# Attention and a gated feed-forward layer in one kernel: first weights cast in row halves on three engines, two gates before two values in tile 0, and a last store of 128 columns

## The chip, the cores and the metric

The kernel runs on one core of a Trainium2 chip. A time is the device time in microseconds (us) of one execution. The kernel before took 367.27 us, the median of 3 runs (366.66 to 367.38). Each timing batch runs the kernel before and the others on the same chip in turn. Each trace is of one execution.

## The reference

Blockwise causal attention (8 batches, 8 heads, 576 positions of 64 elements) is followed by a gated feed-forward layer. Cut to what matters:

```python
scores = (q @ k.T) / 8            # masked: 64-row block i sees blocks j <= i
x = softmax(scores) @ v           # regrouped to 4608 tokens x 512
gate = maximum(x @ w_gate, 0)     # 512 x 1536
val  = x @ w_val                  # 512 x 1536
out  = (gate * val) @ w_out       # 1536 x 512, float32
```

## The kernel before

All inputs are float32 in memory, and the products run in bfloat16. The 4608 tokens form nine tiles of 512. Tiles 0 to 7 are the first 512 positions of a batch; tile 8 gathers the last 64 positions of all batches. TensorE (PE) runs a hand-made order in which attention of later batches is woven between products of the current tile. What bears on the change is the start, where PE must wait for inputs and weights, and the end.

The casts of the weights: a *half* holds 256 of the 1536 columns, for gate and value. One tile is 128 partitions x 4 row chunks x 256 columns, 512 KB as float32. GpSimd (POOL) casts each whole.

```python
def load_w_half(i, g):
    ...                                    # cut: one DMA each for wg and wv, 512 KB
    sts.append((dst[i][:, :, 256 * g : 256 * g + 256], st))
    return sts

def cast_w(sts, eng):
    for dst, st in sts:
        eng(dst, st)
```

The products of a tile come from a generator; each `next` emits one matmul, 512 columns wide. Tiles 0 and 1 start with f = 0 and 1 together, so that chunk c, which comes from head pair c, is wanted late. The rest of the tile takes one f at a time, four gate products and then four value products. PSUM, where products accumulate, has three buffers in `psum_ffn`, one in `psum_one` and two in `psum_sc`.

```python
for f in range(first, 12):
    gate = psum_ffn.tile([128, 512], FP, name="ffnp")
    val = psum_ffn.tile([128, 512], FP, name="ffnp")
    steps = [(t, c) for t in range(2) for c in range(4)]
    if (j, f) == (0, 8):
        steps.sort(key=lambda e: e[1] // 2)
    for t, c in steps:
        product((gate, val)[t], t, c, f)
        if (t, c) == (0, 3):
            gate_sb = relu(gate)           # ScalarE (ACT), 0.60 us
        if (t, c) == (1, 3):
            hidden(gate_sb, val)           # VectorE (DVE), writes hT
        yield
```

The start of the program. The head pairs are counted from 0. `both_av(3)` is the product with v of the fourth pair (pair 3), `to_xT_pe(3, ..)` transposes its result, and the c = 3 products need that.

```python
cast_w(w_0[0][:1], pool)
corners(3, zero_pool)
cast_w(w_0[0][1:], pool)
ffn(4)
to_xT_pe(2, act)
both_av(3)
ffn(5)
to_xT_pe(3, dve)
cast_w(w_0[1], pool)
...
ffn(23)
```

The end. The last output group of tile 8 is cut in two column halves. Each evacuation (`ob`) is followed by two stores of 64 rows, one issued by ACT and one by SyncE (SP).

```python
def outs(j):
    full = [(s, 0, 512) for s in range(4)]
    return full if j < B else full[:3] + [(3, 0, 256), (3, 256, 512)]
```

The softmax here doesn't subtract the row's maximum and nothing guards it: scores larger than these inputs give would overflow.

## Time and profile before

| reading | view | value |
|---|---|---|
| span of the profiled run | page | 364.3 us |
| PE busy, PE's share of the chain | page | 97%, 88% |
| four 512-column matmuls, start to start | timeline of PE | 0.864 us |
| first product of the feed-forward layer | timeline of PE | 16.72 us |
| product f = 10 of tile 0 | timeline of PE | 35.79 us |
| third output group of tile 0 | timeline of PE | 48.37 us |
| evacuation of the last output columns starts | timeline of DVE | 360.47 us |

These are lines of the page of the kernel before: busy time of engines with their share of the span, the clock granted to TensorE in 40 slices (tenths of full speed), shares of the chain that ended last, and the group of the gate products.

```profile
PE 354.9 (97%) x2963; PEld 175.8 (48%) x2963; DVE 168.7 (46%) x393; ACT 168.4 (46%) x278; POOL 113.7 (31%) x147
...
PEclk9999999999999999999999999999999999999999
...
PE 88%; DMA 6%; ACT 2%; DVE 2%; issue 0%; POOL 0%; ACTq 0%
...
L585 PE MATMUL ffnp<-xT,wg 128*128 128x512 bf16 x384 | 103.6, 380 | 0.4 <-POOL wg L340 0.3
```

PE is busy nearly all the time, and PE work makes up nearly all of the chain. The group's idle time before it is only 0.4 us in all, for 384 recorded matmuls. So there is little to gain, and it lies in single gaps. The next lines are from the timeline of PE of the kernel before. Columns: start (us), duration of the row (us), engine, source line, operation, output and inputs, shapes, count. A bracket at the end gives the idle time before the row and what ended it.

```profile
15.97 0.47 PE L508 MATMUL ffnp<-v_bf,attnT 128*128 128x65 bf16 x10
16.72 1.04 PE L585 MATMUL ffnp<-xT,wg 128*128 128x512 bf16 x4 [0.29 <-POOL wg L340]
...
20.58 0.59 PE L585 MATMUL ffnp<-xT,wg 128*128 128x512 bf16 x2
...
21.22 0.38 PE L585 MATMUL sc<-xT,wv 128*128 128x512 bf16 x1
21.64 1.02 PE L585 MATMUL ffnp<-xT,wg 128*128 128x512 bf16 x4
22.58 1.04 PE L585 MATMUL ffnp<-xT,wv 128*128 128x512 bf16 x4
...
32.95 0.59 PE L585 MATMUL ffnp<-xT,wg 128*128 128x512 bf16 x2
33.62 0.60 PE L585 MATMUL ffnp<-xT,wv 128*128 128x512 bf16 x2
...
35.79 0.38 PE L585 MATMUL ffnp<-xT,wg 128*128 128x512 bf16 x1
...
48.37 0.59 PE L646 MATMUL ffnp<-wo,hT 128*128 128x512 bf16 x2 [0.17 <-DVE ob L656]
```

Four gaps can be read. (1) The first product, at 16.72, waits for POOL's cast of wg. (2) The third gate starts at 21.64, where the single product before it (21.22, at 0.216 a product) ended its turn at 21.44. (3) The values that follow start at 22.58, and the four gates before them need only 0.864 from 21.64, so to 22.50. (4) The row at 33.62 comes 0.67 after the row at 32.95, which has two products and needs 0.43. Later, at 48.37, the third output group waits 0.17 for DVE.

The end, from the timeline of DVE of the kernel before, shows the last three evacuations:

```profile
357.85 0.69 DVE L656 COPY ob<-ffnp 128x512 f32<-128x512 f32 x1 [1.90 <-PE ffnp L646]
359.16 0.42 DVE L656 COPY ob<-ffnp 128x256 f32<-128x256 f32 x1 [0.62 <-PE ffnp L646]
360.47 0.42 DVE L656 COPY ob<-ffnp 128x256 f32<-128x256 f32 x1 [0.89 <-PE ffnp L646]
```

### The profile page before, as it was taken

How to read it: one execution, taken by the hardware profiler on the slowest of the kernel's cores; microseconds unless marked ns; L12 is line 12 of the kernel's file. 1: busy time of each engine (PE TensorE's matmuls, PEld its weight loads, DVE VectorE, ACT ScalarE, POOL GpSimd, SP SyncE). 2: the span in 40 equal slices, each digit the busy share in tenths (PEclk: the TensorE clock that was granted, in tenths of full speed). 3: DMA queues.
4: the chain of work that ended last, by engine and by line, in shares of the span. 5: the costliest groups of instructions: out<-in, count | busy, mean ns of one | idle time of the engine just before them, and what ended most of it. 6: DMA issues, size and time to landing. Idle time of an engine off the chain costs nothing.

```text
span 364.3 us, 7455 instructions
## 1 busy us (share of the span) xinstructions
PE 354.9 (97%) x2963; PEld 175.8 (48%) x2963; DVE 168.7 (46%) x393; ACT 168.4 (46%) x278; POOL 113.7 (31%) x147
## 2 busy tenths in 40 slices
PE   6899999999999999999999999999999999999995
PEld 2544455544545445444544454445544454444443
DVE  4744455475534553454454434543455434333332
ACT  4833564677146634664256624564355333302310
POOL 6756656489129100850058003900000000000000
PEclk9999999999999999999999999999999999999999
DMA  7999999999999962999379963999100320020013
GB/s 253 287 356 375 315 248 298 251 94 139 154 183 142 144 144 81 81 134 175 113 50 141 142 146 53 137 127 167 64 17 14 74 81 0 0 88 29 0 45 102
DMA packets 150340, 49.58 MB, mean 136 GB/s; under 512 B 132769, under 2 KB 143265, under 8 KB 150305
## 3 DMA queue, kind: packets, MB, share of 16 engines
q0 software_dynamic: 70320, 8.85, 52.1%
q1 hardware_dynamic: 74704, 31.08, 41.3%
q10 hardware_dynamic: 5280, 9.18, 7.8%
q8 instruction: 23, 0.38, 0.4%
q14 instruction: 13, 0.10, 0.1%
HBM read 37.75 MB, written 9.44 MB: 130 GB/s over the span
## 4 chain that ended last, share of the span: by engine, by line
PE 88%; DMA 6%; ACT 2%; DVE 2%; issue 0%; POOL 0%; ACTq 0%
PE ffnp L585 47%; PE ffnp L646 26%; PE ffnp L508 5%; PE sc L395 3%; PE ffnp L488 3%; DMA stage<-in_moe_w_gate_dram 3%; DMA stage<-in_moe_w_val_dram 3%; PE one L395 2%; ACT attnT L368 1%; PE sc L429 1%; DMA stage<-in_q_dram 1%; DVE qTm L248 1%; PE ffnp L239 0%; PE one L429 0%; ACT kTm L248 0%
## 5 line engine op out<-in xcount | busy, mean ns | idle before, releaser
L601 DVE TENSOR_TENSOR hT<-gate_sb,ffnp 128x512 bf16<-128x512 bf16 x106 | 72.7, 686 | 95.7 <-PE ffnp L585 76.8
L595 ACT ACTIVATE gate_sb<-ffnp 128x512 bf16<-128x512 f32 x108 | 64.8, 602 | 100.0 <-PE ffnp L585 99.9
L585 PE MATMUL ffnp<-xT,wg 128*128 128x512 bf16 x384 | 103.6, 380 | 0.4 <-POOL wg L340 0.3
L646 PE MATMUL ffnp<-wo,hT 128*128 128x512 bf16 (+1 forms) x444 | 101.4, 374 | 0.2 <-DVE ob L656 0.2
L585 PE MATMUL ffnp<-xT,wv 128*128 128x512 bf16 x376 | 101.0, 380 | 0.1
L585 PEld LDWEIGHTS <-wg 128*128 128x128 bf16 x432 | 40.1, 98 | 46.6 <-issue 3.7
L585 PEld LDWEIGHTS <-wv 128*128 128x128 bf16 x432 | 39.7, 98 | 46.0 <-issue 2.3
L646 PEld LDWEIGHTS <-hT 128*128 128x128 bf16 x444 | 40.8, 98 | 42.0 <-issue 1.1
L404 ACT ACTIVATE attnT<-sc 128x1024 bf16<-128x1024 f32 x56 | 57.0, 1042 | 0.0
L282 POOL DMA_DIRECT2D q_bf<-in_q_dram x20 | 18.2, 930 | 94.2 <-DVE hT L601 80.2
L656 DVE COPY ob<-ffnp 128x512 f32<-128x512 f32 (+1 forms) x37 | 25.0, 677 | 41.4 <-PE ffnp L646 41.3
L508 PEld LDWEIGHTS <-attnT 128*128 128x128 bf16 x640 | 26.0, 98 | 14.4 <-DVE xnat L474 3.8
L473 DVE RECIPROCAL recip<-ffnp 128x4 f32<-128x4 f32 (+1 forms) x73 | 13.1, 179 | 35.1 <-PE ffnp L508 23.4
L508 PE MATMUL ffnp<-v_bf,attnT 128*128 128x65 bf16 x570 | 26.4, 194 | 0.0
L410 ACT ACTIVATE attnT<-one 128x256 bf16<-128x256 f32 x28 | 10.7, 384 | 32.6 <-PE ffnp L395 30.1
L474 DVE TENSOR_TENSOR xnat<-ffnp,recip 128x256 bf16<-128x256 f32 x57 | 24.2, 424 | 2.0
L282 POOL DMA_DIRECT2D v_bf<-in_v_dram x25 | 21.4, 944 | 0.0
L450 ACT ACTIVATE attnTt<-one 64x256 bf16<-64x256 f32 x8 | 3.0, 377 | 36.0 <-PE ffnp L429 36.0
L282 POOL DMA_DIRECT2D k_bf<-in_k_dram x20 | 17.8, 942 | 0.0
L395 PE MATMUL sc<-qTm,kTm 64*128 64x512 bf16 (+1 forms) x168 | 17.2, 305 | 0.4 <-ACT kTm L248 0.4
L395 PEld LDWEIGHTS <-kTm 64*128 64x128 bf16 x224 | 9.2, 94 | 16.2 <-issue 11.7
L441 ACT ACTIVATE attnTt<-sc 128x1024 bf16<-128x1024 f32 x16 | 15.7, 1016 | 0.0
(89 smaller groups left out, 241.3 us busy)
## 6 DMA issues: line engine op xcount, KB each, us to landing
out_dram<-ob ACTq DMA_DIRECT2D x32, 256.0 KB, 2.5
stage<-in_moe_w_gate_dram SPq DMA_DIRECT2D x6, 512.0 KB, 9.0
stage<-in_moe_w_val_dram SPq DMA_DIRECT2D x6, 512.0 KB, 9.1
stage<-in_moe_w_out_dram SPq DMA_DIRECT2D x6, 512.0 KB, 10.5
q_bf<-in_q_dram POOLq DMA_DIRECT2D x20, 128.0 KB, 4.6
k_bf<-in_k_dram POOLq DMA_DIRECT2D x20, 128.0 KB, 5.7
v_bf<-in_v_dram POOLq DMA_DIRECT2D x20, 128.0 KB, 5.9
stage<-in_v_dram SPq DMA_DIRECT2D x19, 128.0 KB, 4.4
```

What stands on the lines that cost most here:

```text
L282: ins = nc.gpsimd.dma_start(dst, src[b, :, 128 * c : 128 * c + n, :].rearrange("h p d -> p h d"),)
L395: nc.tensor.matmul(where[c].rearrange("p (c n) -> p c n", n=128), kTm[b % 2][head_of(hh), c, hp, :], qTm[b % 2][head_of(hh), c:4, hp, :], ...
L404: return lambda: nc.scalar.activation(at[:, :, lo : lo + 512], sc, AF.Exp, scale=scale)
L441: return lambda: nc.scalar.activation(at[:, :, 2 * i : 2 * i + 2, 0:256], main[i].rearrange("p g (h n) -> p g h n", h=2), AF.Exp, scale=scale,
L473: nc.vector.reciprocal(recip, av[:, :, 64])
L474: nc.vector.tensor_tensor(out=out, in0=av[:, :, 0:64], in1=recip.to_broadcast([rows, n, 64]), op=AX.mult,)
L508: nc.tensor.matmul(av[:, p, :], at[:, col : col + 128], v_bf[b % 2][:, c, h, :], start=(p == 0), stop=(c == p), skip_group_check=True,)
L585: nc.tensor.matmul(to, (wg, wv)[t][f // 4][:, c, 128 * (f % 4) : 128 * (f % 4) + 128], x[:, c], start=(c == 0), stop=(c == 3),)
L595: nc.scalar.activation(gate_sb, gate, AF.Relu)
L601: nc.vector.tensor_tensor(out=h, in0=gate_sb, in1=val, op=AX.mult)
L646: nc.tensor.matmul(op, hT[f][:, 128 * s : 128 * (s + 1)], wo[f // 4][:, f % 4, n0:n1], start=(f == 0), stop=(f == 11),)
L656: nc.vector.tensor_copy(ob, op)
```

## The change

The intent is to close the four gaps and to shorten the end. (a) The first weights are cast in row halves, by POOL, DVE and ACT together, so that the first products wait for half a cast. (b) Tile 0 takes the gates of two f first and their values then, with one of the four accumulators in the `one` buffer; at f = 8 the eight products of rows 0 and 1 come before the eight of rows 2 and 3. (c) Head pair 3 is handled one product earlier or later: `ffn(5)` becomes `ffn(6)`, and its transposes move one product later. (d) The last columns are cut 384 + 128 and not 256 + 256.

```diff
+    def row_halves(w):
+        dst, st = w
+        return [(dst[:, c : c + 2], st[:, c : c + 2]) for c in (0, 2)]
...
+            pairs = []
+            if j == 0:
+                pairs = [(f, (range(4),)) for f in (2, 4, 6)] + [(8, ((0, 1), (2, 3)))]
+                first = 10
+            for f0, parts in pairs:
+                acc = {
+                    (t, f): psum_one.tile([128, 512], FP, name="one")
+                    if (t, f) == (0, 0)
+                    else psum_ffn.tile([128, 512], FP, name="ffnp")
+                    for t in range(2)
+                    for f in range(2)
+                }
+                gates = []
+                for cs in parts:
+                    for t in range(2):
+                        for f in range(2):
+                            for c in cs:
+                                product(acc[t, f], t, c, f0 + f)
+                                if c == 3 and t == 0:
+                                    gates.append(relu(acc[t, f]))
+                                if c == 3 and t == 1:
+                                    hidden(gates[f], acc[t, f])
+                                yield
...
-                steps = [(t, c) for t in range(2) for c in range(4)]
-                if (j, f) == (0, 8):
-                    steps.sort(key=lambda e: e[1] // 2)
-                for t, c in steps:
+                for t, c in [(t, c) for t in range(2) for c in range(4)]:
...
-        return full if j < B else full[:3] + [(3, 0, 256), (3, 256, 512)]
+        return full if j < B else full[:3] + [(3, 0, 384), (3, 384, 512)]
...
-        cast_w(w_0[0][:1], pool)
+        (gate_01, gate_23), (val_01, val_23) = [row_halves(w) for w in w_0[0]]
+        cast_w([gate_01], pool)
         corners(3, zero_pool)
-        cast_w(w_0[0][1:], pool)
+        cast_w([gate_23], dve)
+        cast_w([val_01], act)
+        cast_w([val_23], pool)
         ffn(4)
         to_xT_pe(2, act)
         both_av(3)
-        ffn(5)
+        ffn(6)
         to_xT_pe(3, dve)
-        cast_w(w_0[1], pool)
+        gate_01, gate_23 = row_halves(w_0[1][0])
+        cast_w([gate_01], act)
+        cast_w([gate_23], pool)
+        cast_w(w_0[1][1:], pool)
...
-        ffn(23)
+        ffn(22)
```

## The prediction

> **What bounds it.** TensorE. The page has PE busy 97% of 364.3 us and gives it 88% of the chain. The Trainium skill ("Perfetto Trace Analysis", Identifying the Most-Contended Engine) warns that PE busy is a poor measure, so I read start-to-start times: in the timeline four 512-column matmuls repeat every 0.864 us, 0.216 each. The skill ("TensorE: Matmul & The Clock Gate", Phases on the wall clock) states the same 216 ns. Stretches at that pitch can't shrink; only gaps between matmuls can. After 60 us the PE waits view shows none. All that matters happens before 48 us, and in the last 4 us.
>
> **Gaps before (timeline, PE).**
> 1. 16.42-16.72: first FFN product waits for POOL's 1024-wide cast of wg (15.62-16.66): 0.29.
> 2. 21.43-21.64: third gate waits for a PSUM buffer that the first relu (20.99, 0.6 us) frees: 0.20.
> 3. 22.50-22.58: waits for the wv cast ending 22.53: 0.08.
> 4. 33.38-33.62: row-half values at f=8 wait for wv casts ending 33.56: 0.24.
> Sum 0.81.
>
> **What the change does.**
> - Casts in row halves cost about 0.62 (POOL, ACT) and 0.43 (DVE) in place of 1.04. The first half ends at about 16.24, so gap 1 goes and the first product starts near 16.43. The other halves land on idle time of DVE (17.14-18.32) and ACT (16.73-18.02).
> - But the c=3 products need xT of pair 3. From its transposes to the first c=3 product took 0.90 (19.68 to 20.58). In between now stand two products, not three. Transposes at 19.59, c=3 at about 20.49: only 0.09 of the 0.29 survives; a new gap of about 0.24 appears before c=3.
> - Gate 2 now takes the "one" buffer, free since 20.4, and its weights are cast by ACT and POOL by 20.6 (DMA lands at 19.95). Gap 2 goes: third gate at about 21.35, before 21.64.
> - Two gates before two values move each wv use 0.86 later: gap 3 goes. f=8 starts at about 31.72 (was 32.09).
> - At f=8, eight products of rows 0-1 come before those of rows 2-3; the late values are wanted at 34.3, cast by 33.56: gap 4 goes. f=10 starts at 35.17 (was 35.79), perhaps 0.05 later, as the relu of f=9 frees its buffer then.
> Gain at f=10: about 0.6.
>
> **Does it survive?** The weight stream doesn't speed up: a cast every 1.36-1.5 us, each ended by a DMA wait. With PE 0.6 sooner, the last wo half (cast ends 45.03) is wanted at 45.5: fits. v of batch 1 (cast ends 47.04) is wanted at 46.8: PE will wait about 0.25. That hides in front of an older wait: output group 3 starts when DVE has evacuated group 2 (48.31 before, 47.7 now). So I expect the whole 0.6 from 48 us on to 360.
>
> **Tail.** Last evacuation: 512 wide 0.69, 256 wide 0.42, so 128 wide about 0.29 (estimate, linear): 0.13 sooner. But the 384-wide store is issued just before, at about 360.4, and an issue holds its queue 0.47-0.5 us, so the last store starts near 360.88 against 360.92. Gain 0.05. PE work there is unchanged (same columns).
>
> **Prediction.** 367.27 - 0.65 = 366.6 us; 366.0 to 367.2. Faster by over 2%: 0.01; within 2%: 0.98; slower: 0.01.
>
> **What would show it.** Timeline, PE: first FFN product near 16.43; gap of about 0.24 before c=3; third gate near 21.35; no gap between 21.4 and 35; f=10 near 35.2; third output group near 47.75; the last evacuation near 360 minus 0.1. The DMA landing times of weights unchanged. Chain: still PE from 34 us on.
>
> **What would make it wrong.** Weights landing later in that run; ACT held by the 19.95 landing so that the first relu slips; POOL and DVE casts slowing each other; a DMA-fed wait after 48 us returning the gain; run-to-run spread (0.7 us), as large as the gain.

## The result, and the profile after

| kernel | median, us | range, us | runs |
|---|---|---|---|
| before | 367.00 | 366.66 to 367.38 | 4 |
| changed | 366.50 | 365.84 to 366.95 | 4 |

The ratio is 0.9985, with a 95% interval from 0.9963 to 1.0006. A ratio here is the mean time of one kernel's runs over that of the other's runs of the same rounds, so it is not quite the ratio of the medians. The predicted time was 366.6.

The profiled run of the changed kernel took 366.81 us with a span of 364.7, which is longer than the 364.3 of the profiled run before. Two lines of its page, the clock and the chain:

```profile
PEclk9899999999999999999999999999999999999999
...
PE 94%; DVE 2%; issue 1%; ACT 1%; POOL 0%; ACTq 0%; POOLq 0%
```

The chain is still PE, now at 94%; the 6% of DMA that the kernel before had in it, waits for weights among them, are gone in this run. They are not gone for good: DMA has 7% in undo_tail and 9% in after_warm (below), where PE comes to the weights earlier. The second slice of the clock line has an 8 where the kernel before had a 9. The view of windows tells more. These lines are from the kernel before, then from the changed kernel, for the stretch from 9 to 10 us: length, busy time and number of instructions of five engines, granted clock, share of DMA time, GB/s.

```profile
9.00:10.00 1.00, 1.00 (x12) 0.62 (x14) 0.27 (x1) 0.76 (x2) 0.77 (x2) 1.00 1.38 224
```

```profile
9.00:10.00 1.00, 1.00 (x10) 0.74 (x8) 0.09 (x1) 0.64 (x2) 0.78 (x2) 0.50 1.38 224
```

In this run of the changed kernel TensorE had half its clock, from 8.59 to 12.00 us by the clock record. Four transposes took 0.61 us there, and 0.40 us in traces at full speed. So PE came to the place of the change 0.94 us later: the last product with v before the feed-forward layer (the second head of pair 2) began at 16.91 where it had begun at 15.97. Runs of the kernel before also show the mean clock of this run, 0.994 (two of 11 in the next batch), so the edit is not what makes such a spell. It hides what the edit did, unless one counts from that product. Timeline of PE, changed kernel:

```profile
16.91 0.47 PE L512 MATMUL ffnp<-v_bf,attnT 128*128 128x65 bf16 x10
17.21 0.97 PE L589 MATMUL ffnp<-xT,wg 128*128 128x512 bf16 x3
...
20.97 0.38 PE L589 MATMUL sc<-xT,wv 128*128 128x512 bf16 x1
21.43 0.59 PE L589 MATMUL ffnp<-xT,wg 128*128 128x512 bf16 x2
...
22.30 1.03 PE L589 MATMUL one<-xT,wg 128*128 128x512 bf16 x4
23.16 0.59 PE L589 MATMUL ffnp<-xT,wg 128*128 128x512 bf16 x2
...
36.15 0.59 PE L589 MATMUL ffnp<-xT,wg 128*128 128x512 bf16 x2
...
48.73 0.59 PE L670 MATMUL ffnp<-wo,hT 128*128 128x512 bf16 x2 [0.17 <-DVE ob L680]
```

Counted from that product with v, f = 10 comes after 36.15 - 16.91 = 19.24 us, and before the change it came after 35.79 - 15.97 = 19.82. That is 0.58 sooner; the prediction had about 0.6. But the two are not quite alike: PE was late here, so the half cast of wg had ended (16.70) before PE wanted it (17.21). A whole cast of 1.04 us, begun at 16.08 like the half, would have ended at 17.12, also in time (an estimate); undo_casts bears this out. The predicted new gap is there: the c = 3 products start at 21.43, and the row at 20.97 was done issuing by 21.19, so 0.24. The third gate goes to `one` at 22.30 without a wait, and two gates run on at the pitch. At f = 10 there is a gap of 0.04.

The end of the changed kernel, from the timeline of DVE, and then the stores that ACT issued after 359.5 us, from the view of the tile `ob` (count; duration in ns as least, median, longest; first and last start):

```profile
358.19 0.69 DVE L680 COPY ob<-ffnp 128x512 f32<-128x512 f32 x1 [1.90 <-PE ffnp L670]
360.14 0.96 DVE L680 COPY ob<-ffnp 128x384 f32<-128x384 f32 x2 [1.26 <-PE ffnp L670]
```

```profile
L579 ACTq DMA_DIRECT2D out_dram<-ob x2: 498/645/792, 360.7 to 361.3; - x2
```

The last two evacuations are printed as one row: 384 columns at 360.14 and 128 columns at 360.81, the latter 0.29 us long, as estimated. It ended at 361.11, so 2.91 after the start of the last full-width evacuation (358.19); before, it was 360.89 - 357.85 = 3.04. That is 0.13 gained. But ACT issued the store of the 384 columns at 360.73, and its last store began only at 361.33 and held the queue 0.79 us. Counted from the last full-width evacuation, ACT's last store began after 3.13 us, and before it had begun after 3.07.

### The profile page after: what moved, and what is told of

Its sections match the earlier page's. It is cut to its first block, busy times and chain, and to the rows that moved or that the text cites. A ratio compares the mean times of both kernels' runs of the same rounds, so it can differ in the third digit from the quotient of the medians.

```text
span 364.7 us, 7410 instructions
## 1 busy us (share of the span) xinstructions
PE 352.6 (97%) x2915; PEld 176.0 (48%) x2963; DVE 168.1 (46%) x394; ACT 169.4 (46%) x280; POOL 113.1 (31%) x147
## 4 chain that ended last, share of the span: by engine, by line
PE 94%; DVE 2%; issue 1%; ACT 1%; POOL 0%; ACTq 0%; POOLq 0%
PE ffnp L589 49%; PE ffnp L670 25%; PE ffnp L512 5%; PE sc L399 3%; PE ffnp L492 3%; PE one L399 2%; PE sc L433 1%; PE one L589 1%; PE ffnp L239 1%; PE ffnp L715 1%; PE sc L356 1%; DVE qTm L248 1%; PE one L433 0%; PE sc L589 0%; PE one L512 0%
## 5 line engine op out<-in xcount | busy, mean ns | idle before, releaser
L599 ACT ACTIVATE gate_sb<-ffnp 128x512 bf16<-128x512 f32 x104 | 62.4, 602 | 93.1 <-PE ffnp L589 93.1
L589 PE MATMUL ffnp<-xT,wv 128*128 128x512 bf16 x367 | 99.0, 379 | 0.5
L670 PE MATMUL ffnp<-wo,hT 128*128 128x512 bf16 (+2 forms) x421 | 98.0, 373 | 1.5 <-DVE ob L680 0.2
L589 PE MATMUL ffnp<-xT,wg 128*128 128x512 bf16 x352 | 96.6, 379 | 0.9
L680 DVE COPY ob<-ffnp 128x512 f32<-128x512 f32 (+2 forms) x37 | 25.0, 677 | 41.1 <-PE ffnp L670 41.0
```

What stands on the lines that cost most here:

```text
L589: nc.tensor.matmul(to, (wg, wv)[t][f // 4][:, c, 128 * (f % 4) : 128 * (f % 4) + 128], x[:, c], start=(c == 0), stop=(c == 3),)
L599: nc.scalar.activation(gate_sb, gate, AF.Relu)
L670: nc.tensor.matmul(op, hT[f][:, 128 * s : 128 * (s + 1)], wo[f // 4][:, f % 4, n0:n1], start=(f == 0), stop=(f == 11),)
L680: nc.vector.tensor_copy(ob, op)
```

## The experiments

Three questions were open. What makes runs of one kernel differ by more than the change? Which parts of the change pay? Is the gain at f = 10 kept to the end, as the prediction said?

Theory at the start: the casts and the pairs together give 0.6 us, kept whole to the end, and the end gives nothing. Rivals: the pairs alone give it; or the gain is lost later; or all differences in total time are clock. Edits below are against the changed kernel, unless stated.

### The changed kernel again (after_again)

No edit.

> The changed kernel unaltered, to see its times beside the mean granted clock of each run. Theory: an early stretch of about 3.4 us at half clock in some runs (granted mean 0.994 instead of 1.000) costs about 0.7 to 0.9 us, independent of the change; among runs at 1.000 it is 0.5 to 0.7 us below the kernel before at 1.000. Rival: the change itself brings the slow stretch, then the kernel before never shows 0.994 and the ratio is near 1.000. If the profile falls at 1.000: first FFN product near 16.4, third gate near 21.35, f=10 near 35.2, third output group near 47.75.

Measured: median 366.13 us (365.77 to 367.70, 6 runs), and for the kernel before 366.95 (366.11 to 368.68, 11 runs). Ratio 0.9989, interval 0.9962 to 1.0016. The runs fall into two bunches: four from 365.77 to 366.20, two at 367.7. The profiled run was one of the latter. Timeline of PE of this run, then of one with the clock up early (before_warm, below):

```profile
11.46 0.61 PE L239 MATMUL ffnp<-ident,q_bf 128*128 128x128 bf16 x4
```

```profile
10.09 0.40 PE L239 MATMUL ffnp<-ident,q_bf 128*128 128x128 bf16 x4
```

The same transposes take 0.61 us in the first and 0.40 in the second, although the mean clock shown for the first run is 1.000. The clock record begins at the first grant, here at 14.03 us, and the mean leaves out what came before. The profiled run of the kernel before was granted full speed at 6.36 us. From the last product with v before the layer to f = 10 it is again 19.24 us, and from 46 us to the end this run lies a steady 1.25 to 1.27 us behind the kernel before (table below), so its delay arose before that. What the edit is worth in such a run isn't shown, as no trace of the kernel before has a late grant. The mean of 0.994, for which the theory looked, doesn't tell the bunches apart: all six runs show 1.000. The rival fails, since the kernel before shows 0.994 too. The Trainium skill ("TensorE: Matmul & The Clock Gate", What's actually happening) tells of a free-running window of 3413 ns after which the clock goes to full or half. The half-speed spell above lasted 3.41 us, which agrees.

### Whole casts on POOL as before (undo_casts)

```diff
-        (gate_01, gate_23), (val_01, val_23) = [row_halves(w) for w in w_0[0]]
-        cast_w([gate_01], pool)
+        cast_w(w_0[0][:1], pool)
         corners(3, zero_pool)
-        cast_w([gate_23], dve)
-        cast_w([val_01], act)
-        cast_w([val_23], pool)
+        cast_w(w_0[0][1:], pool)
...
-        gate_01, gate_23 = row_halves(w_0[1][0])
-        cast_w([gate_01], act)
-        cast_w([gate_23], pool)
-        cast_w(w_0[1][1:], pool)
+        cast_w(w_0[1], pool)
```

> Changed kernel with the whole-tile POOL casts of before. Theory (prediction): the first product waits for the 1024-wide cast again, everything up to f=10 shifts by 0.29 us at equal clock, so 0.3 us slower than the changed kernel in runs of the same clock. Rival: the casts give only the 0.09 us that the xT wait leaves, so under 0.1 us slower. In the trace: from the start of the first product (wg) to the third gate 4.9 us or less.

Measured: median 367.74 us (366.30 to 369.12), ratio 1.0019, interval 0.9986 to 1.0052. Inconclusive: half of the six runs took 368.7 us or more. The profiled run (368.74) got its clock only at 17.53 us. PE was then so late that the weights were there, and f = 10 came 19.24 us after the product with v, exactly as with halves. The first product to the third gate took 5.08 us, and not the 4.9 expected; in the profiled run of the changed kernel, which was late too, it is 5.08 as well. The run shows only that half casts are worth nothing when PE is late.

### Gate, value, gate, value as before, half casts kept (undo_pairs)

```diff
-            pairs = []
-            if j == 0:
...                                        # cut: the whole block of the pairs goes
-                for t, c in [(t, c) for t in range(2) for c in range(4)]:
+                steps = [(t, c) for t in range(2) for c in range(4)]
+                if (j, f) == (0, 8):
+                    steps.sort(key=lambda e: e[1] // 2)
+                for t, c in steps:
```

> Changed kernel with gate, value, gate, value for tile 0 as before, half-cast weights kept. Theory: gaps 2, 3 and 4 return (0.20 + about 0.08 + 0.24), so 0.4 to 0.55 us slower than the changed kernel at the same clock, and almost as slow as before. Rival: with earlier weights the gaps stay closed, difference under 0.1 us. In the trace: a gap of about 0.2 us before the third gate and about 0.25 us before the last values of f=8.

Measured: median 367.39 us (366.58 to 367.97), ratio 1.0015, interval 0.9990 to 1.0039. The profiled run had its clock at 4.74 us. Timeline of PE:

```profile
21.35 1.02 PE L589 MATMUL ffnp<-xT,wg 128*128 128x512 bf16 x4
22.66 1.04 PE L589 MATMUL ffnp<-xT,wv 128*128 128x512 bf16 x4 [0.29 <-POOL wv L340]
...
33.03 0.59 PE L589 MATMUL ffnp<-xT,wg 128*128 128x512 bf16 x2
33.70 0.60 PE L589 MATMUL ffnp<-xT,wv 128*128 128x512 bf16 x2
```

The gaps are back. The third gate waits from 21.15 to 21.35, the values of f = 2 wait 0.29 for the cast of wv, and at f = 8 there is a gap again (33.03 to 33.70 for two products). f = 10 came at 35.86, 20.22 us after the product with v. In the trace of the changed order with an equally early clock (undo_tail, below) it came at 35.04, after 19.46. So the pairs are worth about 0.76 to 0.82 us at that place, about as much as the whole change gains at f = 10, for without the pairs the half casts only let PE run into these gaps sooner. The total isn't read: four of the six runs show 0.994, the half-speed spell.

### Transposes of pair 3 one product sooner (xT3_sooner)

```diff
-        ffn(6)
+        ffn(5)
...
-        ffn(22)
+        ffn(23)
```

> Changed kernel with the transposes of pair 3 one product earlier (5 products, then transposes, as before). Theory: in the changed kernel the tensor engine waits 0.24 us for xT of pair 3 before the c=3 products; with three products between, this gap goes and the kernel is 0.2 us faster at the same clock. Rival: the transposes then wait for xnat of pair 3, and the gap only moves (0 us).

Measured: median 366.62 us (366.59 to 366.88), ratio 0.9991, interval 0.9969 to 1.0013. Timeline of PE:

```profile
21.02 0.38 PE L589 MATMUL sc<-xT,wv 128*128 128x512 bf16 x1
21.26 0.59 PE L589 MATMUL ffnp<-xT,wg 128*128 128x512 bf16 x2
```

The c = 3 products follow 0.24 after the product before them, against 0.46 in the changed kernel. f = 10 came 19.03 us after the product with v, 0.21 sooner than with `ffn(6)`. So part (c) of the change costs 0.2 us at this place. The total doesn't show it: most of these runs have a mean clock of 0.994 or 0.995, so they probably had a half-speed spell, as their profiled run did.

### Keeping the clock up: the kernel before (before_warm) and the changed kernel (after_warm)

Theory: the spread within a kernel is the grant of the clock at the start. Rival: it is DMA. The edit gives PE dummy products in the idle times before 10 us, and makes the first of them independent of the identity matrix that POOL builds.

```diff
-    def junk(n):
-        jp = psum_ffn.tile([128, 512], FP, name="ffnp")
+    def junk(n, cols=512):
         for _ in range(n):
-            nc.tensor.matmul(jp, ident, zeros, start=True, stop=True)
+            nc.tensor.matmul(
+                jp[:, 0:cols], zeros[:, 0:128], zeros[:, 0:cols], start=True, stop=True
+            )
...
-        junk(7)
+        jp = psum_one.tile([128, 512], FP, name="one")
+        junk(8)
...                                        # junk(1) after pe_mains(0), junk(2) before part(1, 0)
```

The same edit was made to both kernels.

> The kernel before, with more dummy matmuls at the start (8 of them, not held by the identity tile, one more after the first transposes and two before the scores of pair 1), so that the tensor engine's clock stays granted from about 5 to 8 us on in every run. Theory: the late or interrupted grant of the clock before 18 us makes the spread (366.1 to 368.7); with it gone all runs lie within 0.4 us, near the fastest seen, 366.1 to 366.4. No lower, as the first FFN product (16.7 us) and the last values of f=8 (33.6 us) wait for weights in DRAM order. Rival: the spread has another cause and stays at 2 us.

> The changed kernel with the same early dummy matmuls. Theory: with the clock granted early in both kernels the predicted gain shows: third gate near 21.3 us, f=10 near 35.2 us, 0.5 to 0.6 us below the kernel before with the dummies, at 365.6 to 365.9. Rival: being earlier, it meets a wait for the weight stream after 36 us (wo, or v of batch 1) and keeps only 0.2 to 0.3 us.

| kernel | median, us | mean, us | range, us | ratio to before | interval |
|---|---|---|---|---|---|
| before, 11 runs | 366.67 | | 366.09 to 368.83 | | |
| before_warm, 6 runs | 366.52 | 366.47 | 365.96 to 366.76 | 0.9986 | 0.9962 to 1.0010 |
| after_warm, 6 runs | 366.00 | 366.21 | 365.78 to 366.87 | 0.9979 | 0.9954 to 1.0004 |

The range of the kernel before shrinks from 2.7 to 0.8 us. In the timed batches of the experiments, 13 of 47 runs of kernels without the dummies took more than 367.5 us, and none of 36 with them (the kernel with the other stores, below, is left out). But 11 of these 13 were on another chip; on the chip of the runs with dummies, 2 of 12 without took so long. The clearer sign are the two long runs that were profiled: both got the clock late, at 14.03 and 17.53 us. So a late grant makes runs long; that it made every long run, and that the dummies prevent it, is likely and not proved, as only profiled runs have the record. The spread didn't shrink to the 0.4 us that was expected. The dummies don't make the kernel before faster than its own good runs. The rival holds in part: in the trace of before_warm the first product still waits 0.76 us for POOL's cast of wg and starts at 17.10, since that weight came later from DMA in this run.

With the clock out of the way, the change is worth 366.47 - 366.21 = 0.26 us by means and 0.52 by medians, where 0.5 to 0.6 was expected. Each kernel's runs still spread by about 1 us, so six runs don't settle a figure between these. Two of the six runs of after_warm took 366.71 and 366.87, the others 365.78 to 366.06.

### The two together (xT3_warm)

Dummies as above, and `ffn(5)`, `ffn(23)`.

> Changed kernel, dummies, and the transposes of pair 3 one product sooner. Theory: 0.21 us sooner at the third gate (as the profiles with a late clock showed, 19.03 against 19.24 us from the last av to f=10) and 0.2 us faster overall than the changed kernel with dummies. Rival: 0, if the weight stream limits f=10 to f=11 or the output products by then.

Measured: median 366.10 us (365.97 to 366.35), mean 366.14, ratio 0.9977, interval 0.9954 to 1.0001. In the trace f = 10 came at 34.79 and the third output group at 47.54, against 35.26 and 48.05 in after_warm. About half of that is not the edit: the first wg landed 0.26 us sooner in this run (15.49 against 15.75). The expected 0.2 us isn't seen in the total: 0.07 us by means, and the median is 0.10 longer.

### The product with v of pair 4 two products later (av_later_warm)

Dummies as above. The changed kernel's PE waits about 0.4 us for the v of batch 1 at 47 us; this moves the product that wants it.

```diff
-        events = round_at(96, 4, (120, 120.1), (125, pe_xT), (6, 11))
+        events = round_at(96, 4, (122, 122.1), (126, pe_xT), (6, 11))
```

> Changed kernel with the early dummy matmuls, and the products with v of pair 4 two output products later. Theory: with an early clock the changed kernel is held at the third output group by the cast of v of batch 1 (cast end plus about 0.65 us: 47.40 to 48.05); two products of 0.216 us now stand before it, so the tensor engine no longer waits 0.4 us for v, and what follows starts 0.1 us (v early) to 0.4 us (v late) sooner than in the changed kernel with dummies. Rival: the wait moves to the next DMA-fed operand, k of batch 1 (cast end about 48.2), and nothing is won.

Measured: median 366.06 us (365.95 to 366.71), mean 366.16, ratio 0.9978, interval 0.9952 to 1.0005. The wait for v is gone from the trace, and tile 1 began at 58.93, against 59.29 in after_warm. The rival holds in part: the next wait, for k of batch 1 at 50 us, grew from 0.32 to 0.45. In total it is again 0.05 us by means, below what these runs resolve.

### Whole casts with the clock kept (undo_casts_warm)

The edit of undo_casts, with the dummies.

> Changed kernel with dummies, but with the whole-tile POOL casts of before. Theory: with an early clock the first FFN product waits for the 1.04 us cast (DMA landing plus 1.1 us, 16.7 to 17.1) in place of the 0.62 us one, so everything to f=10 is 0.3 to 0.45 us later than in the changed kernel with dummies, and f=10 starts at 35.5 to 35.8; in total 0 to 0.4 us slower, as the cast of v at 47 us may hide it. Rival (the earlier run without dummies, whose profile had a late clock): no difference at all.

Measured: median 366.32 us (365.98 to 367.00), mean 366.37, ratio 0.9980, interval 0.9954 to 1.0006. In the trace the first product started at 16.64 and f = 10 at 35.43; with half casts f = 10 started at 35.26 (after_warm) and 35.04 (undo_tail). So half casts are worth 0.2 to 0.4 us at f = 10 when the clock is early. The difference in total, 0.16 us by means, is within the spread. The profiled run (367.00) also waited 0.8 us at 59 us for data that came late by DMA, which no other trace here shows, so its later part is not used below.

### The change without its end (undo_tail)

```diff
-        return full if j < B else full[:3] + [(3, 0, 384), (3, 384, 512)]
+        return full if j < B else full[:3] + [(3, 0, 256), (3, 256, 512)]
```

> Changed kernel with the last group split 256 + 256 as before; read in the trace, as 0.06 us is below what times can show. Theory: the tail part of the change alone costs 0.06 us, so from the start of the third 512-column copy of the last tile to the end of the span it takes 6.43 us, as in the kernel before, against 6.49 in the changed one, with the last ACT store starting 0.03 us after its copy. Rival: the 0.06 us come from elsewhere, and it stays at 6.49.

No rounds: 366.33 us, and 366.26 for the kernel before. Its clock came at 4.86 us, so this is the trace in which parts (a) to (c) can be read as the prediction meant them. Timeline of PE:

```profile
16.25 1.04 PE L589 MATMUL ffnp<-xT,wg 128*128 128x512 bf16 x4 [0.21 <-POOL wg L340]
...
21.18 1.03 PE L589 MATMUL one<-xT,wg 128*128 128x512 bf16 x4
...
35.04 1.02 PE L589 MATMUL ffnp<-xT,wg 128*128 128x512 bf16 x4
...
47.22 0.77 PE L512 MATMUL ffnp<-v_bf,attnT 128*128 128x65 bf16 x20 [0.39 <-POOL v_bf L181]
47.83 0.59 PE L670 MATMUL ffnp<-wo,hT 128*128 128x512 bf16 x2
```

The first product is at 16.25 (predicted 16.43), the third gate at 21.18 (21.35), f = 10 at 35.04 (35.17), the third output group at 47.83 (47.7). The wait for v is 0.39 (0.25). At f = 10 the gain is 0.75, and at 48 us it is 48.37 - 47.83 = 0.54 us: the wait for v took back 0.21. As for the end, the last store of ACT started 0.03 us after its evacuation, as expected, but the measure took 6.47 us and not 6.43 (table at combined). The next question is where the gain is at 360 us. The evacuations of output groups are good marks, for each kernel has the same 37 (the next to last one, whose width the change moves, is left out):

| start of evacuation, less that of the kernel before | tile 0, groups 1 to 4 (46 to 60 us) | next (94.5 us) to the end |
|---|---|---|
| undo_tail | -0.75, -0.75, -0.54, -0.54 | -0.09 to -0.11 |
| after_warm | -0.53, -0.53, -0.31, -0.30 | +0.29 to +0.31 |
| xT3_warm | -1.00, -1.00, -0.83, -0.83 | -0.45 |
| av_later_warm | -0.67, -0.67, -0.66, -0.66 | -0.36 |
| combined | -0.88, -0.88, -0.53, -0.53 | -0.11 to -0.13 |
| after (half-speed spell) | about +0.36 | +0.34 |
| after_again (late clock) | about +1.27 | +1.26 |

Where PE comes early, 0.3 to 0.6 us is given back between 60 and 94 us (0.2 in one_store_warm, which isn't in the table), and nothing after. Where PE comes 0.2 us late or more, nothing changes in that stretch. The place is near 75 us, at the scores of batch 2; undo_tail and after_warm lose another 0.11 and 0.14 at 80 us, again at a PSUM buffer that DVE frees. These are lines of the kernel before, timeline of DVE and then of PE:

```profile
72.87 2.12 DVE L223 COPY qTm<-perm 128x512 bf16<-128x512 bf16 x2
74.92 0.67 DVE L601 TENSOR_TENSOR hT<-gate_sb,ffnp 128x512 bf16<-128x512 bf16 x1
75.51 0.59 DVE L223 COPY qTm<-perm 128x512 bf16<-128x512 bf16 x1
```

```profile
75.65 0.28 PE L395 MATMUL one<-qTm,kTm 64*128 64x256 bf16 x1
```

And of undo_tail, in the same order:

```profile
72.34 2.47 DVE L223 COPY qTm<-perm 128x512 bf16<-128x512 bf16 x2
74.73 0.67 DVE L605 TENSOR_TENSOR hT<-gate_sb,ffnp 128x512 bf16<-128x512 bf16 x1
```

```profile
75.12 0.28 PE L399 MATMUL one<-qTm,kTm 64*128 64x256 bf16 x1
75.46 0.27 PE L399 MATMUL ffnp<-qTm,kTm 64*128 64x256 bf16 x1
```

In undo_tail the last products before the scores ended early enough for the scores to start at 75.12 instead of 75.65. Then PE stopped after one matmul until 75.46: the next one needs a PSUM buffer, which DVE frees by the hidden product that runs from 74.73 to 75.41. DVE came to it late, since its two copies of qTm before took 2.47 us, and 2.12 in the kernel before. The copy at 75.51 in the kernel before took 0.59; POOL had nothing under way when it began. In after_warm the pair took 2.62, the hidden product began at 75.11, and the trace names it as what ended PE's wait of 0.21 at 75.83.

What makes the copies slow can be read from POOL's casts of v of batch 2 beside them. Timeline of POOL in undo_tail, then POOL and DVE in the late run of the changed kernel (after):

```profile
72.94 1.43 POOL L189 CAST v_bf<-stage 128x1024 bf16<-128x1024 f32 x1
```

```profile
72.18 3.07 POOL L189 CAST v_bf<-stage 128x1024 bf16<-128x1024 f32 x2
73.23 1.10 DVE L223 COPY qTm<-perm 128x512 bf16<-128x512 bf16 x2
```

In undo_tail the second copy took 1.44 us and ended at 74.81, 0.45 after POOL's cast beside it (74.36). In each trace of the upper five rows of the table, and of the kernel before, the second copy took 1.44 to 1.45 us and ended 0.45 to 0.46 after a POOL cast. In the late run it is the other way round: both copies took 0.59, and POOL's second cast beside them 2.09 in place of 1.04. So the two engines took turns. The Trainium skill ("SBUF — State Buffer", SBUF: two separate sides) states that DVE, in some of its operations, and POOL share a pair of ports, which the one that starts first locks for its whole instruction. These traces agree, though none records the lock itself. POOL's own work moves with the arrival of data: its cast of k of batch 2 started at 64.51 before, 66.54 in undo_tail and 66.88 in after_warm, each after a wait for DMA. No run here took POOL's work away from that stretch, so what the return would be without it is not shown.

So a PE that is early finds DVE no earlier there, because DVE follows POOL and POOL follows DMA. What is left at the end then depends on when data arrive in that run; that is inferred from these few traces. A check by estimate: 366.29 (the profiled run of the kernel before) plus the last column of the table gives 366.6 for after_warm and 366.2 for undo_tail, and their profiled runs took 366.71 and 366.33. By the same sum the four shorter runs of after_warm, near 365.93, kept about 0.4 us. So the return is probably not the same in all runs, though those runs have no trace.

### The last two stores as one transfer each (one_store_warm)

In place of two transfers of 64 rows for each piece, ACT stores the 384 columns and SP the 128, each as one transfer whose target has batch as the outermost dimension, of size 2. Against xT3_warm.

```diff
+            if s == 3:
+                (nc.scalar, nc.sync)[n0 > 0].dma_start(
+                    out.rearrange("(b s) n -> b s n", s=S)[6:8, 512:576, n0:n1], ob
+                )
+                return
```

> As xT3_warm, and the two last stores as one DMA each: 384 columns on the ACT queue, the last 128 on the SP queue. Theory: in the changed kernel the last store of ACT starts 0.20 us after its copy ended (361.33 against 361.10 + 0.03), held by the issue of the 384-column store on the same queue, and takes 0.79 us to issue; on a queue of its own it starts 0.03 us after the copy, and the span ends 0.2 to 0.35 us sooner. Rival: landing sets the end, then under 0.1 us.

Measured: median 371.32 us (370.94 to 372.11), ratio 1.0120, interval 1.0092 to 1.0147. That is 5 us worse. The row of SP's last store in the timeline of SP, and the rate of all DMA from 360 to 370 us, from the view of DMA (GB/s in 40 slices of 0.25 us):

```profile
360.44 0.62 SPq L578 DMA_DIRECT2D out_dram<-ob  x1
```

```profile
GB/s 361 172 0 0 0 25 25 25 31 43 12 37 37 43 18 49 49 45 47 49 47 49 49 49 49 49 49 43 43 43 43 0 0 0 0 0 0 0 0 0
```

The store began at 360.44, 0.03 after the evacuation ended, so the queue was free as the theory wanted. But the transfers then crept at 50 GB/s or less until about 367.8 us, and the span ended at 369.3. The Trainium skill ("DMA: Bandwidth & Descriptors", Rules for kernel authors) warns that an outermost dimension under 16 confines a transfer to at most that many DMA engines. This trace agrees: from 362 to 367 us the share of DMA time is 0.13 to 0.14 of 16 engines, about two engines' worth. Two stores of 64 rows landed in 2.0 and 2.2 us in the kernel before, and these still moved data over 7 us after they were issued. The question of the queue is left as it was, and the trial is a miss.

### All that helped, with an end of 352 + 160 columns (combined)

xT3_warm, av_later_warm, and the cut moved to 352:

```diff
-        return full if j < B else full[:3] + [(3, 0, 384), (3, 384, 512)]
+        return full if j < B else full[:3] + [(3, 0, 352), (3, 352, 512)]
```

> Changed kernel, dummies, transposes of pair 3 one product sooner, products with v of pair 4 two later, and the last group split 352 + 160 columns instead of 384 + 128. Theory: the last ACT store then starts within 0.05 us of its copy, and from the third 512-column copy of the last tile to the end of the span it takes 6.3 us (6.43 before, 6.49 changed); in all 0.3 to 0.5 us below the changed kernel with dummies, 365.4 to 365.8, the fastest of all. Rival: the DMA stream holds the tensor engine at k of batch 1 and the total equals the changed kernel with dummies less 0.15 us.

Measured: median 365.86 us (365.60 to 366.77), mean 365.99, ratio 0.9973, interval 0.9948 to 0.9998. It is the fastest of all by its median, though not apart from after_warm by more than the spread, and the only faster one whose interval leaves out 1, if barely, and by far less than 2%. Timeline of DVE at the end:

```profile
360.34 0.33 DVE L680 COPY ob<-ffnp 128x160 f32<-128x160 f32 x1 [0.30 <-PE ffnp L670]
```

ACT's last store was issued at 360.70, 0.03 after the evacuation ended at 360.67, although its issue still took 0.75 us. A measure of the end that no earlier stage disturbs is the time from the start of the last full-width evacuation to the end of the span:

| end | kernels | us |
|---|---|---|
| 256 + 256 | before, before_warm, undo_tail | 6.43, 6.43, 6.47 |
| 384 + 128 | after, after_again, after_warm, xT3_warm and five more | 6.46 to 6.50 |
| 352 + 160 | combined | 6.24 |

So 384 + 128 gives nothing and may cost some hundredths, while 352 + 160 gives 0.2 us, in one trace. The wide piece must be early enough for its store to leave the queue before the narrow piece is ready.

## Why the prediction was right, and which of its terms were not

**The time: right.** It said 366.6 us and "within 2%" at 0.98; measured was 366.5. The agreement of the medians to 0.1 us is partly luck, as the medians of the kernel before were 367.27, 367.00, 366.95 and 366.67 from batch to batch.

**"Gain at f=10: about 0.6": right.** In undo_tail, where the first wg landed when it had before (15.53 and 15.57 us), it was 35.79 - 35.04 = 0.75. PE began that stretch 0.39 earlier there, which let the first product start 0.18 before the predicted 16.43; less that, it is about 0.57 (an estimate). The 0.58 of the profiled run agrees in part by luck, since PE was late and half casts are worth nothing then. The gaps closed where the prediction said: no wait for wv near 22.5, third gate in `one`, no gap at f = 8. undo_pairs brought the latter three back.

**The new gap before c = 3, "about 0.24": right.** It was 0.24, and xT3_sooner removed 0.21 of it.

**The wait for v, "about 0.25", hidden in front of an older wait: right in kind, short in size.** It was 0.39 in undo_tail and 0.40 in after_warm. It hid only in part: the older wait of 0.17 at the third output group went, but the gain shrank from 0.75 at f = 10 to 0.54 there (0.53 to 0.31 in after_warm).

**"So I expect the whole 0.6 from 48 us on to 360": wrong, where PE is early.** undo_tail and after_warm gave back 0.45 and 0.6 us near 75 and 80 us, where PE met PSUM buffers that DVE frees, and DVE had been held up by POOL's casts and copies. The step that failed was the reading that, after 60 us, no listed wait of PE means slack. DVE ended its hidden product at 75.59 in the kernel before and PE began the scores at 75.65: they met without a listed wait, but there was no slack in it. The prediction had named "a DMA-fed wait after 48 us returning the gain" among the risks and gave it no term in the sum.

**The end, "Gain 0.05": not there, though the mechanism was right.** The narrow evacuation took 0.29 as estimated, and the queue was held as foreseen. But ACT's second issue took 0.79 and not 0.50, and the end took 6.46 to 6.50 us in place of 6.43 to 6.47, so no gain.

**The sum of 0.65.** The mis-sized term is what reaches the end. With the clock kept, the change gave 0.26 us by means and 0.52 by medians.

**Spread.** The prediction knew of 0.7 us between runs and not of its cause. It is up to 2.7 us, and much of it is the clock at the start: the two long runs that were profiled got it late. A late clock also takes away what the half casts gain, since PE then comes after the weights.

**Still open:** how much of the gain would last if POOL's work were moved away from 75 us, why the weights' arrival varies from run to run, and how much each part gives in total, which is below what six runs resolve.

## What to carry to other kernels

When an engine with no listed waits runs earlier, look for the places where its inputs were ready only just in time: the chain of waits doesn't list them, but they take the gain back. Before explaining a difference of under 1%, count each trace from a common event past the start, and check instruction durations for a cold clock, because a mean clock of 1.000 can hide one. When a last store is made narrow, balance it against the time for which the store before it holds the queue.

## What the Trainium skill lacked or had wrong

- "TensorE: Matmul & The Clock Gate" (What's actually happening) puts the penalty of the warm-up under 1% of a typical span and advises against fitting a count of slow products. Here it is under 1% too, up to 2.7 us between runs of the kernel before, but that is several times the effect under study. The grant came at 4.8 to 17.5 us over the traces of these kernels, and at 4.9 to 6.6 in the seven with dummy products. The page doesn't tell how busy PE must be within a window of 3.41 us to keep full speed. Counted from these 14 traces (ends of products are modelled), the clock fell in mid-run after two windows, with PE busy for 2.04 us (after) and 2.03 (xT3_sooner), and after none with 2.22 or more.
- The same page (Back-to-back issue gap) gives about 131 ns per matmul of 512 columns as sustained with a weight load before each. This kernel's stream, which has such loads, holds 216 ns (0.864 us for four), which agrees with the figure of 216 that the page calls isolated.
- "DMA: Bandwidth & Descriptors" is right about a small outermost dimension (one store of 2 x 64 rows for each piece made the kernel 5 us longer), but I found there no figure for how long an issue holds its queue when another follows: 0.47 to 0.50 us for one, and 0.79 for ACT's last in the 384 + 128 end (0.75 in the 352 + 160 end).
